# Computing the low halves of the second MLP's weights on VectorE in place of GpSimd

## The chip, the cores and the metric

The kernel runs on one core of one Trainium2 chip. The metric is the device time of one execution in microseconds (us), less is better; a kernel's number is the median of several runs.

## The reference

Three layers follow each other. The first is banded attention, with a window of 32 keys in half of the heads and a dilated window in the others. The second is a maxout MLP, the third an MLP with a rational activation. All is in float32.

```python
attn = softmax(where(mask, q @ k.T / 8, -1e9)) @ v      # 4 x 8 heads, 576 x 64 each
x = attn as (2304, 512)
h = maximum(maximum(x @ w1, x @ w2), x @ w3)            # 512 -> 768
x2 = h @ w_out                                          # 768 -> 512
h = x2 @ w_in                                           # 512 -> 2048
g = (a0 + a1*h + a2*h**2 + a3*h**3) / (1 + |b0|*|h| + |b1|*h**2 + 1e-6)
out = g @ w_out2                                        # 2048 -> 512
```

## The kernel before

To keep the precision, every matrix of the two MLPs is split into a high half, rounded to a format that TensorE takes at full rate, and a low half, the rest. A product is three matmuls: high by high, high by low, low by high. `mm3` (L497 to L499) issues such triples.

The tokens of the attention and the first MLP go in six units of 384 tokens (`TU`). While TensorE does the first MLP of unit u (`moe1`, L502), the pieces of the attention of unit u+1 are put between its groups. A group is 12 matmuls into one of three PSUM banks; ScalarE copies the first of three groups out (L514), VectorE takes the maximum with the second and third (L516), and then ScalarE writes the high half hh (L520) and VectorE the low half hl (L521). The result goes through xs (L530) to the DRAM tile x2d (the transfer of L531 is issued by GpSimd).

During those units the weights of the second MLP are converted from the input's 64-bit words to float32 and put into the DRAM tiles w2d. In the last unit they come back and are split. That is `load_w2` (L537): a transfer on SP's queue into one of five slots w2r (L542), a copy on ScalarE that makes the high half of the weight tile w2s (L544), and a subtraction that makes the low half (L545). It is called 32 times: five times at the start of the last unit, three times after each of the six f groups of the first MLP (into memory that the weights of that group leave free), and nine times at the end (into memory that the rest of the first MLP leaves free). `load_x2` (L550) brings one of the six blocks of 384 tokens of x2 from x2d into x2r (L552, on SP's queue), and `split_x2` (L556) splits it on ScalarE (L558) and VectorE (L559).

The second MLP goes in 96 slices: six blocks of tokens by sixteen slices of 128 of the 2048 columns. For each slice, `stage_h` makes h in one of five PSUM tiles (12 matmuls, L497 to L499 again, with w2s and x2h, x2l). `act_a` (L718 to L720, ScalarE) and `dve_a` (L725, L727, L728, VectorE) read it; L728 is the last reader of the PSUM tile. `act_b` (L734, L735) and `dve_b` (L740, L742, L744) finish the rational function, `act_c` (L750) and `dve_c` (L755) split it into gh and gl, and `stage_o` (L767 to L769) adds nine matmuls to the output.

The order on each engine is set by a scheduler that works through priorities: the program's order, apart from stretches that are marked as later ones (`load_w2` in the last unit by 300 places, `load_x2` and `split_x2` by 200). Each engine then takes its instructions strictly in that order, and each of them waits for what it needs.

Of the kernel before, what the change touches and what calls it, by code (L numbers as in the profile page):

```python
# [7 lines left out]
F32 = mybir.dt.float32  # L8
# [84 lines left out]
def kernel(  # L93
# [17 lines left out]
    nc = tc.nc  # L111
# [425 lines left out]
    def load_w2(pool):  # L537
        i = n2[0]
        n2[0] += 1
        _, side, c = order2[i]  # L540
        r = w2r_p.tile([128, 512], F32, tag="w2r", bufs=W2R, name="w2r")
        nc.sync.dma_start(out=r, in_=w2d[i])  # L542
        t = pool.tile([128, 1024], F32R, tag=f"w2_{i}", name=f"w2s{i}")
        nc.scalar.activation(out=t[:, 0:512], in_=r, func=AF.Copy)  # L544
        nc.gpsimd.tensor_sub(t[:, 512:1024], r, t[:, 0:512].bitcast(F32))  # L545
        w2s[side, c] = t

    x2 = {}
# [12 lines left out]
    with ExitStack():  # L561
# [69 lines left out]
        for u in range(NU):  # L631
            last = u == NU - 1
            pieces = attn(u + 1) if not last else iter(())
            if last:
                while cv:
                    cv_tick(len(conv_seq))
                cv_es[0].close()
                at_es.close()
                x2_p = ctx.enter_context(
                    tc.tile_pool(name="x2", bufs=1, side="right", reuse_waits="tile"))  # L640
                w2r_p = ctx.enter_context(
                    tc.tile_pool(name="w2r", bufs=1, side="right", reuse_waits="tile"))
                w2a = ctx.enter_context(
                    tc.tile_pool(name="w2a", bufs=1, side="right", reuse_waits="tile"))
                with tc.high_priority(offset=-LATE_X2):
                    load_x2(0)
                with tc.high_priority(offset=-LATE_W2):
                    for _ in range(W2A):
                        load_w2(w2a)
            slot = 0  # L650
            groups = moe1(u)
            while True:
                if u == 0:
                    cv_tick(n_w1)
                    while cv_at["lo"] < (n_w1 if slot >= 3 * F1 else slot + AHEAD):
                        cv_tick(n_w1)
                group = next(groups, None)
                if group is None:
                    break
                kind, f, j = group  # L660
                slot += 1
                if u == 0:
                    pass
                elif not last:
                    tick += 1
                    if tick * TICK // 88 > (tick - 1) * TICK // 88:
                        with tc.high_priority(offset=-LATE_CV):
                            cv_tick(len(conv_seq))
                next(pieces, None)
                if last:  # L670
                    if slot in (8, 10, 12, 14):
                        with tc.high_priority(offset=-LATE_X2):
                            split_x2(0, (slot - 8) // 2)
                    if kind == "h" and j == 2:
                        w1_es[f].close()
                        w2b = ctx.enter_context(
                            tc.tile_pool(name=f"w2b{f}", bufs=1, side="right",
                                         reuse_waits="tile"))
                        with tc.high_priority(offset=-LATE_W2):
                            for _ in range(3):  # L680
                                load_w2(w2b)
# [14 lines left out]
        while n2[0] < len(order2):  # L696
            load_w2(w2c)
# [83 lines left out]
        for g in range(NSL + 3):  # L781
            t, c = divmod(g, F2)
# [122 lines left out]
```

## Time and profile before

| what | value |
|---|---|
| median of three runs | 824.51 us (822.74 to 827.67) |
| the profiled execution's own time | 822.7 us |
| its span, first to last instruction | 820.9 us |
| mean granted TensorE clock | 0.987 of full speed |
| TensorE busy | 801.5 us |
| VectorE busy | 612.2 us |
| ScalarE busy | 486.6 us |
| GpSimd busy | 81.7 us |

In the rows below PE is TensorE's matmuls, PEld its weight loads, DVE is VectorE, ACT ScalarE, POOL GpSimd, SP the engine that issues most transfers; a q behind a name is the engine's sequencer. L545 is line 545 of the kernel. Times are in us from the start of the span unless a column says ns. An arrow in brackets names what ended the idle time ahead of an instruction.

### The profile page before, as it was taken

The numbers are of one execution on the slowest core, as the hardware profiler recorded it, in microseconds if no ns is written. First come the engines' busy times: TensorE is split into PE (matmuls) and PEld (weight loads), VectorE is DVE, ScalarE is ACT, GpSimd is POOL, SyncE is SP. The second block draws the span as 40 slices with busy tenths as digits, with TensorE's granted clock in tenths as the row PEclk, the third lists the DMA queues.
The fourth block names the chain that finished last, engine by engine and source line by source line (L and its number), as shares of the span: only waits on it lengthen the run. The fifth ranks groups of instructions, "written<-read, shape, count | busy, mean of one in ns | idle before, by whom it ended". The sixth has DMA issues, their size and how long they took to land.

```text
span 820.9 us, 13079 instructions
## 1 busy us (share of the span) xinstructions
PE 801.5 (98%) x4965; PEld 745.0 (91%) x4965; DVE 612.2 (75%) x1152; ACT 486.6 (59%) x1023; POOL 81.7 (10%) x109
## 2 busy tenths in 40 slices
PE   7899999999999999999989999999999999999998
PEld 5699999999999999998978899999999999999996
DVE  3589666565566566544199899999999999998996
ACT  3677533333333333255378787787788778777775
POOL 0000000100110110048440000000000000000000
PEclk9699999999999999999989999999999999999999
DMA  8787336565465544426410011011002001000001
GB/s 264 243 315 254 121 122 194 183 197 167 154 191 164 162 153 142 153 68 210 153 52 1 0 40 39 1 40 39 1 1 78 1 0 39 1 2 28 11 1 39
DMA packets 29439, 82.54 MB, mean 101 GB/s; under 512 B 3904, under 2 KB 7488, under 8 KB 29376
## 3 DMA queue, kind: packets, MB, share of 16 engines
q1 hardware_dynamic: 24080, 64.66, 25.0%
q0 software_dynamic: 5296, 17.04, 5.5%
q8 instruction: 39, 0.64, 0.3%
q14 instruction: 24, 0.20, 0.1%
HBM read 63.87 MB, written 17.83 MB: 100 GB/s over the span
## 4 chain that ended last, share of the span: by engine, by line
PE 90%; DMA 3%; ACT 2%; issue 2%; DVE 1%; POOL 1%; SPq 0%; ACTq 0%; POOLq 0%
PE mm L497 11%; PE mm L498 11%; PE mm L499 11%; PE acc L769 8%; PE acc L767 8%; PE acc L768 8%; PE h L497 8%; PE h L498 8%; PE h L499 8%; PE sc L287 3%; PE tpp L343 2%; PE pv L369 2%; DMA w1r<-in_w_dram 2%; PE pv L363 1%; DMA mk<-in_masks_dram 1%
## 5 line engine op out<-in xcount | busy, mean ns | idle before, releaser
L497 PE MATMUL mm<-x1h,w1s 128*128 128x384 f32 x432 | 147.9, 344 | 1.8 <-ACT m L514 0.9
L498 PE MATMUL mm<-x1l,w1s 128*128 128x384 f32 x432 | 145.9, 338 | 1.0 <-DVE x1l L385 1.0
L499 PE MATMUL mm<-x1h,w1s 128*128 128x384 f32 x432 | 145.3, 336 | 0.0
L497 PE MATMUL h<-x2h,w2s 128*128 128x384 f32 x384 | 130.3, 339 | 3.8 <-DVE p L728 3.8
L498 PE MATMUL h<-x2l,w2s 128*128 128x384 f32 x384 | 130.4, 340 | 0.0
L499 PE MATMUL h<-x2h,w2s 128*128 128x384 f32 x384 | 130.3, 339 | 0.0
L767 PE MATMUL acc<-w2s,gh 128*128 128x512 f32 x288 | 113.7, 395 | 0.0
L768 PE MATMUL acc<-w2s,gh 128*128 128x512 f32 x288 | 113.4, 394 | 0.0
L769 PE MATMUL acc<-w2s,gl 128*128 128x512 f32 x288 | 110.3, 396 | 0.0
L718 ACT ACTIVATE q<-h 128x384 f32<-128x384 f32 x96 | 47.2, 492 | 79.2 <-PE h L499 76.9
L725 DVE SCALAR_TENSOR_TENSOR q<-q,cs,ab 128x384 f32<-128x384 f32 x96 | 67.8, 706 | 29.4 <-ACT ab L719 29.3
L497 PEld LDWEIGHTS mm<-x1h,w1s 128*128 128x128 f32 x432 | 81.3, 189 | 3.0 <-ACT m L514 1.3
L498 PEld LDWEIGHTS mm<-x1l,w1s 128*128 128x128 f32 x432 | 81.6, 189 | 2.3 <-DVE x1l L385 2.3
L499 PEld LDWEIGHTS mm<-x1h,w1s 128*128 128x128 f32 x432 | 81.4, 188 | 0.0
L497 PEld LDWEIGHTS h<-x2h,w2s 128*128 128x128 f32 x384 | 73.1, 190 | 8.0 <-DVE p L728 4.1
L498 PEld LDWEIGHTS h<-x2l,w2s 128*128 128x128 f32 x384 | 72.9, 190 | 3.8
L499 PEld LDWEIGHTS h<-x2h,w2s 128*128 128x128 f32 x384 | 73.0, 190 | 0.3
L516 DVE TENSOR_TENSOR m<-mm,m 128x384 f32<-128x384 f32 x72 | 39.9, 555 | 41.1 <-PE mm L499 34.7
L769 PEld LDWEIGHTS acc<-w2s,gl 128*128 128x128 f32 x288 | 54.2, 188 | 11.9
L720 ACT ACTIVATE p<-h,cs 128x384 f32<-128x384 f32 x96 | 65.0, 677 | 0.0
L734 ACT ACTIVATE r<-q,cs 128x384 f32<-128x384 f32 x96 | 59.6, 620 | 5.2 <-DVE q L725 4.7
L768 PEld LDWEIGHTS acc<-w2s,gh 128*128 128x128 f32 x288 | 54.2, 188 | 9.3
(86 smaller groups left out, 1492.7 us busy)
## 6 DMA issues: line engine op xcount, KB each, us to landing
w1r<-in_w_dram SPq DMA_DIRECT2D x18, 512.0 KB, 7.7
raw<-in_w_in_dram SPq DMA_DIRECT2D x16, 512.0 KB, 3.7
w2d<-cvt POOLq DMA_DIRECT2D x32, 256.0 KB, 3.0
raw<-in_w_out_dram SPq DMA_DIRECT2D x16, 512.0 KB, 3.7
w2r<-w2d SPq DMA_DIRECT2D x32, 256.0 KB, 3.1
qTp<-in_qp_dram SPq DMA_DIRECT2D x12, 384.0 KB, 4.1
qTd<-in_qd_dram SPq DMA_DIRECT2D x12, 384.0 KB, 4.6
x2d<-xs POOLq DMA_DIRECT2D x24, 192.0 KB, 2.6
```

The costliest lines, as they stand in the source:

```text
L287: nc.tensor.matmul(scs[n // G][:, n % G, :], lhsT=lq, rhs=rk, start=not pem, stop=not pem or n % G == G - 1)
L497: nc.tensor.matmul(o, lhsT=lh, rhs=rh, start=(i == 0), stop=False)
L498: nc.tensor.matmul(o, lhsT=lh, rhs=rl, start=False, stop=False)
L499: pe_at[0] = nc.tensor.matmul(o, lhsT=ll, rhs=rh, start=False, stop=(i == n - 1))
L516: nc.vector.tensor_tensor(out=t, in0=o, in1=t, op=ALU.max)
L718: nc.scalar.activation(out=s["q"], in_=s["h"], func=AF.Square)
L720: nc.scalar.activation(out=s["p"], in_=s["h"], func=AF.Identity, scale=cs[:, 3:4], bias=cs[:, 2:3])
L725: nc.vector.scalar_tensor_tensor(out=s["q"], in0=s["q"], scalar=cs[:, 5:6], in1=s["ab"], op0=ALU.mult, op1=ALU.add)
L734: nc.scalar.activation(out=s["r"], in_=s["q"], func=AF.Ln, scale=LS, bias=cs[:, 6:7])
L767: nc.tensor.matmul(o, lhsT=gh, rhs=w[:, 0:512], start=(c == 0), stop=False)
L768: nc.tensor.matmul(o, lhsT=gh, rhs=w[:, 512:1024], start=False, stop=False)
L769: nc.tensor.matmul(o, lhsT=gl, rhs=w[:, 0:512], start=False, stop=(c == F2 - 1))
```

## The change

The subtraction that makes the low half of a weight tile of the second MLP is issued on VectorE instead of on GpSimd. Nothing else is edited; the scheduler orders the instructions anew.

```diff
@@ -542,7 +542,7 @@
         nc.sync.dma_start(out=r, in_=w2d[i])
         t = pool.tile([128, 1024], F32R, tag=f"w2_{i}", name=f"w2s{i}")
         nc.scalar.activation(out=t[:, 0:512], in_=r, func=AF.Copy)
-        nc.gpsimd.tensor_sub(t[:, 512:1024], r, t[:, 0:512].bitcast(F32))
+        nc.vector.tensor_sub(t[:, 512:1024], r, t[:, 0:512].bitcast(F32))
         w2s[side, c] = t
```

## Rows read from the trace of the kernel before

**Rows 1.** The page's busy times (busy us, share, instructions) and its chain.
```profile
PE 801.5 (98%) x4965; PEld 745.0 (91%) x4965; DVE 612.2 (75%) x1152; ACT 486.6 (59%) x1023; POOL 81.7 (10%) x109
...
PE 90%; DMA 3%; ACT 2%; issue 2%; DVE 1%; POOL 1%; SPq 0%; ACTq 0%; POOLq 0%
```

**Rows 2.** Windows: length, busy us of PE, PEld, DVE, ACT, POOL, clock, DMA.
```profile
355.00:408.00 53.00, 50.97 (x290) 49.97 (x291) 22.24 (x28) 23.78 (x48) 32.77 (x26) 1.00 0.51 157
...
420.00:422.00 2.00, 0.00 (x0) 0.00 (x0) 1.97 (x4) 1.01 (x3) 0.54 (x1) 0.81 0.00 0
422.00:424.00 2.00, 1.87 (x6) 1.87 (x7) 1.96 (x5) 2.00 (x4) 0.00 (x0) 0.50 0.04 8
```

**Rows 3.** Timeline of TensorE (start, duration, what), 407 to 431.
```profile
407.76 0.34 PE L497 MATMUL h<-x2h,w2s 128*128 128x384 f32 x1
...
417.99 0.34 PE L499 MATMUL h<-x2h,w2s 128*128 128x384 f32 x1
422.13 0.69 PE L497 MATMUL h<-x2h,w2s 128*128 128x384 f32 x1 [3.80 <-DVE p L728]
...
428.06 0.35 PE L497 MATMUL h<-x2h,w2s 128*128 128x384 f32 x1
...
429.46 0.39 PE L767 MATMUL acc<-w2s,gh 128*128 128x512 f32 x1
...
430.16 0.40 PE L769 MATMUL acc<-w2s,gl 128*128 128x512 f32 x1
```

**Rows 4.** VectorE: timeline 411 to 428, and L725's group over the span.
```profile
411.94 9.02 DVE L725 SCALAR_TENSOR_TENSOR q<-q,cs,ab 128x384 f32<-128x384 f32 x1 [14.05 <-ACT ab L719]
420.88 0.55 DVE L727 TENSOR_TENSOR p<-h,p 128x384 f32<-128x384 f32 x1
...
427.09 0.55 DVE L755 TENSOR_TENSOR gl<-p,gh 128x384 fp32r<-128x384 f32 x1
...
L725 DVE SCALAR_TENSOR_TENSOR q<-q,cs,ab 128x384 f32<-128x384 f32 x96 | 67.8, 706 | 29.4 <-ACT ab L719 29.3
```

**Rows 5.** Timeline of GpSimd, 380 to 421.
```profile
380.39 10.98 POOL L545 TENSOR_TENSOR w2s<-w2r,w2s 128x512 fp32r<-128x512 f32 x8 [3.56 <-ACT w2s L544]
...
409.30 11.24 POOL L545 TENSOR_TENSOR w2s<-w2r,w2s 128x512 fp32r<-128x512 f32 x9
```

**Rows 6.** L521 and L516, 355 to 410 (ns: minimum/median/maximum; first, last start).
```profile
L521 DVE TENSOR_TENSOR hl<-m,hh x6: 558/1292/1641, 365.8 to 396.6; 128x384 fp32r<-128x384 f32 x6
...
L516 DVE TENSOR_TENSOR m<-mm,m x12: 545/557/558, 359.9 to 395.5; 128x384 f32<-128x384 f32 x12
```

**Rows 7.** Lines L545 and L480 over the span, the same columns.
```profile
L545 POOL TENSOR_TENSOR w2s<-w2r,w2s x32: 1250/1290/1611, 359.9 to 419.3; 128x512 fp32r<-128x512 f32 x32
...
L480 DVE TENSOR_TENSOR w1s<-cvt,w1s x18: 647/686/694, 27.7 to 81.7; 128x512 fp32r<-128x512 f32 x18
```

**Rows 8.** Timelines of SP, TensorE and ScalarE, 373 to 381.
```profile
373.07 0.52 SPq L552 DMA_DIRECT2D x2r<-x2d  x1
...
375.28 0.45 PE L497 MATMUL mm<-x1h,w1s 128*128 128x384 f32 x1 [0.93 <-ACT m L514]
...
378.02 1.77 ACT L558 ACTIVATE x2h<-x2r 128x384 fp32r<-128x384 f32 x4 [2.80 <-DMA x2r<-x2d]
...
380.60 0.45 PE L497 MATMUL mm<-x1h,w1s 128*128 128x384 f32 x1 [0.86 <-DVE m L516]
```

**Rows 9.** Waits (total us, times, longest us) from 335, and w2r's landing times.
```profile
ACT w2s L544 <- DMA w2r<-w2d: 7.8, 5, 2.3
...
SPq L542 <- POOL w2s L545: 56.1, 26, 16.3
...
DMA to landing us min/median/max: 2.6/3.1/6.4
```

**Rows 10.** Timeline of ScalarE, the last of 32 high halves.
```profile
417.12 0.63 ACT L544 ACTIVATE w2s<-w2r 128x512 fp32r<-128x512 f32 x1
```

## The prediction

> **What bounds the kernel now.** First the page's busy shares and chain [rows 1]: TensorE is busy for 801.5 of 820.9 us and owns 90% of the chain that ended last. So a change on VectorE or GpSimd moves the time only where TensorE stands still or runs slowly. The next view is the windows around the hand-over between the two MLPs [rows 2]. From 355 to 408 TensorE is busy for 50.97 of 53 us; in 420 to 422 it does nothing, and then its clock is granted at 0.50, the 1.2 GHz level of the two (1.2 and 2.4).
>
> The timeline of TensorE shows the hole [rows 3]. The second MLP's first matmul starts at 407.76, the sixtieth (five slices of 12) at 417.99, so full-speed spacing is 10.23 / 59 = 0.173 us. The next starts at 422.13, released by VectorE's L728, the last reader of slice 0's PSUM tile (there are five such tiles). From there 18 matmuls take until 428.06, 0.329 us each. After that the spacing is the full-speed one again.
>
> Why was L728 late? On VectorE, L725 of slice 0 starts at 411.94 and lasts 9.02 us, where the other 95 average (67.8 - 9.02) / 95 = 0.62 [rows 4]. On GpSimd, nine subtractions run without a break from 409.30 to 420.54 [rows 5], and L725 ends 0.42 us after them. Other VectorE instructions with two SBUF inputs suffer too: L521 in this stretch has a median of 1.29 us and a maximum of 1.64 against a minimum of 0.56, while L516, one of whose inputs is in PSUM, keeps 0.55 to 0.56 [rows 6]. GpSimd's eight in a row from 380.39 took 10.98 / 8 = 1.37 each, the nine only 11.24 / 9 = 1.25 [rows 5]: there VectorE got turns in between, here none. I read this as the two engines excluding each other while both read SBUF.
>
> The Trainium skill's "SBUF — State Buffer", section "Who interferes with whom", says that a VectorE instruction with two SBUF inputs contends with a GpSimd one that reads SBUF, and that the one issued first keeps the shared ports for its whole instruction while the second blocks. By that rule L725 should have waited for one subtraction, not for seven; the sum by it is that of the second rival below. The trace agrees for L521 and not for L725.
>
> **Step 1, the hole at 418.** Without GpSimd's subtractions L725 takes 0.62 and slice 0's tile is free by about 414, before TensorE asks for it at 418.2. Removed: 422.13 - 417.99 - 0.17 = 3.97 us of standstill, and 5.93 - 18 x 0.173 = 2.81 us of half clock [rows 3]; together 6.8.
>
> **Step 2, what VectorE takes over.** It gets 32 subtractions of 128x512. L480 does the same on the same shape and types in 0.686 us at the median, against 1.29 on GpSimd [rows 7]; 32 x 0.686 = 22 us. All but the nine above, 23, fall into 355 to 408: 15.8 us on top of 22.2 busy (which the exclusion inflates), 38 of 53 [rows 2]. The cover is TensorE's 51 us of matmuls there; if it went, all 15.8 would count. The other nine, 6.2 us, come after 409.3, because their tiles lie in memory that the first MLP frees last. By the first low half of the output, VectorE must also do 14 instructions, from L725 to L755 of slice 0; 12 of these steps took from 420.88 to 427.09, 0.52 us each [rows 4], so 7.3 us. 409.3 + 6.2 + 7.3 = 422.8. Three stage-a groups wait for ScalarE; apart from the long wait of 14.05 these waits sum to 29.3 - 14.05 over 95, 0.16 us each [rows 4], 0.5 for three: 423.3. TensorE reaches the output matmuls after 84 at 407.76 + 84 x 0.173 = 422.3 and wants the low half with the fourth of them, 0.7 us later as from 429.46 to 430.16 [rows 3], so at 423.0. Given back: 0.3 us, between 0 (VectorE hides all) and 6.0 (the first rival). I take 0.3, as each of its terms is a row of just these instructions.
>
> **Step 3, two smaller holes.** TensorE stood 0.93 us at 375.28, behind ScalarE's L514, and 0.86 at 380.60, behind VectorE's L516 [rows 8]. ScalarE's copies of the high halves wait for w2r transfers, 7.8 us in five waits; SP issues those only when a subtraction frees one of five slots, and waits 56.1 us for GpSimd in 26 waits [rows 9]. The second hole hangs on the same slots: SP comes to the x2r load only at 373.07, ScalarE goes on with its data at 378.02, and L516 stands behind that on VectorE [rows 8]. A subtraction on VectorE frees its slot some 0.6 us sooner, eight in a row several us sooner, and SP's queue moves up with them; an issue 1.0 us earlier is enough for the second hole. I take both, 1.8 us; the bounds are 0 and 1.8. Where a slot comes free early, what is late next is the release of the weight tiles by TensorE itself.
>
> **Moved queues.** GpSimd keeps only transfer issues, those of x2d among them, which follow ScalarE's xs and gain nothing. SP's two kinds of load move up. The new wait on VectorE is for ScalarE's L544; behind it stand L516 and stage a, and TensorE waits for both.
>
> **Sum.** The profiled execution took 822.7 (its span is 820.9): 822.7 - 6.8 - 1.8 + 0.3 = 814.4. The median of the three runs, 824.5, is 1.8 above it; for a median I add half of that: **815.3 us**. About 0.5% (4.1 us) is what a measurement of this kernel can tell from no change; the border is 820.4.
>
> **Rivals.**
> *VectorE becomes the late one at the hand-over.* If all nine last subtractions stand before L725 of slice 0 in VectorE's order, it starts after the ninth high half, 417.12 + 0.63 [rows 10], plus 0.69: 418.4. The low half is then ready at 418.4 + 7.3 + 0.5 = 426.2, 3.2 us late, and if the clock falls as it did after 3.97 us of standstill, 2.8 more: 814.4 - 0.3 + 6.0 = 820.1, as a median 821.0. For it: the program asks for these loads ahead of stage a. Against: four of the nine come late, and stage a of slice 0 is ready between them. Chance 0.12.
>
> *L725's wait is not GpSimd's doing beyond one instruction.* Then only 1.25 us of it goes and the rest has a cause that stays: 822.7 - 1.25 - 1.8 = 819.6, as a median 820.5. For it: L521 got through between eight subtractions that ran in a row, in 1.64 at most. Against: L725 ends as GpSimd ends. Chance 0.08.
>
> *Slower: VectorE blocked behind late transfers.* A w2r transfer lands up to 6.4 us after its issue [rows 9], most likely behind an x2r load, whose own data took 4.95 (373.07 to 378.02). Add 0.63 and 0.69, and VectorE is held until 7.7 us after the issue if a subtraction stands ahead of an L516 on its queue. The first MLP has three PSUM banks, so TensorE can run two more groups, 24 x 0.173 = 4.2 us; then it stands 3.5 us and loses 2.8 of clock, 6.3 a time. It decides from the point where a transfer is issued less than 3.5 us before VectorE comes to its subtraction. Twice makes 814.4 + 12.6 = 827.0, as a median 827.9. For it: the hole of 0.86 us is this pattern in small, behind x2r [rows 8]. Against: the slots come free sooner. Chance 0.06.
>
> **Numbers.** Forecast 0.74. Faster by over 0.5%: nearly all of the forecast and half of the second rival, which sits on the border: 0.76. Within 0.5%: the first rival, half of the second and a little of the forecast: 0.18. Slower: 0.06. Range 813 to 822: below, both savings with nothing given back and no offset (814.1), less 1 us for the scatter of the runs; above, the first two rivals with 1 us for the same. The third is left out.
>
> **What would show it.** Right: no L725 above 1 us, L521 near 0.56 throughout, no TensorE gap and no clock of 0.50 between 418 and 428, 32 subtractions of 0.69 us on VectorE, x2r issued before 372. Wrong: a TensorE gap of over 2 us at the first output matmuls, released by L755 (first rival); an L725 that still lasts several us (second); L516 waiting for L544 with TensorE idle behind it (third). What would make the forecast fail as a whole is an order of instructions on VectorE that the trace of before can't show.

## The result, and the profile after

The changed kernel takes **814.33 us** (median of four runs, 814.25 to 815.14) against 824.17 for the kernel before beside it (822.74 to 827.67). The ratio is 0.9877, with a 95% interval from 0.9857 to 0.9897: 9.8 us, 1.2%, faster. The forecast was 815.3, in a range of 813 to 822. The profiled execution is the one of 815.14 us; its span is 813.4, its mean granted clock 0.991.

First the page's busy times and its chain, to be set beside [rows 1].

```profile
PE 800.1 (98%) x4965; PEld 745.1 (92%) x4965; DVE 614.1 (76%) x1184; ACT 487.9 (60%) x1023; POOL 39.2 (5%) x77
...
PE 96%; ACT 1%; DVE 1%; DMA 1%; issue 0%; SPq 0%; POOL 0%; ACTq 0%
```

VectorE has 32 instructions more and GpSimd 32 fewer, yet VectorE is busy for only 1.9 us more (614.1 for 612.2): its subtractions cover 21.0 us, and what it no longer spends is for the most part time in which its instructions had stood kept waiting, counted as busy: 8.7 us at L725 (67.8 to 59.1, as its group below shows), 4.0 at L521 and 3.9 at L559. TensorE's share of the chain went from 90% to 96%.

The windows of [rows 2], on the kernel after:

```profile
355.00:408.00 53.00, 52.76 (x345) 52.39 (x341) 28.47 (x51) 25.95 (x51) 2.18 (x5) 1.00 0.48 159
420.00:422.00 2.00, 2.00 (x12) 1.94 (x12) 2.00 (x5) 1.97 (x5) 0.00 (x0) 1.00 0.01 4
422.00:424.00 2.00, 2.00 (x10) 1.66 (x9) 2.00 (x5) 2.00 (x6) 0.00 (x0) 1.00 0.00 0
```

TensorE is busy throughout at the hand-over, and the granted clock stays at 1.00, the 2.4 GHz level, where it had been 0.50. Next VectorE's timeline at the hand-over, which answers to [rows 4], with the first low half of the output, L755:

```profile
408.24 3.10 DVE L545 TENSOR_TENSOR w2s<-w2r,w2s 128x512 fp32r<-128x512 f32 x5 [10.70 <-ACT w2s L544]
411.25 0.61 DVE L725 SCALAR_TENSOR_TENSOR q<-q,cs,ab 128x384 f32<-128x384 f32 x1
411.78 0.55 DVE L727 TENSOR_TENSOR p<-h,p 128x384 f32<-128x384 f32 x1
412.41 0.69 DVE L545 TENSOR_TENSOR w2s<-w2r,w2s 128x512 fp32r<-128x512 f32 x1
413.02 0.61 DVE L728 SCALAR_TENSOR_TENSOR p<-p,co,h 128x384 f32<-128x384 f32 x1
...
421.18 0.55 DVE L755 TENSOR_TENSOR gl<-p,gh 128x384 fp32r<-128x384 f32 x1
```

L725 of slice 0 takes 0.61 us in place of 9.02. Five of the nine last subtractions stand ahead of it on VectorE, as one block of 3.10 us; the other four come between the steps of stage a. TensorE's timeline at the first output matmuls shows whether that was too much:

```profile
421.38 0.34 PE L499 MATMUL h<-x2h,w2s 128*128 128x384 f32 x1
421.56 0.39 PE L767 MATMUL acc<-w2s,gh 128*128 128x512 f32 x1
...
422.73 0.63 PE L769 MATMUL acc<-w2s,gl 128*128 128x512 f32 x2
```

L755 ends at 421.18 + 0.55 = 421.73, and TensorE comes to the first matmul that reads gl at 422.73: 1.0 us to spare, and no wait. The moved instruction itself, the low halves hl of the first MLP, and L725's group (busy us, mean ns, idle before), to be set beside [rows 6], [rows 7] and [rows 4]:

```profile
L545 DVE TENSOR_TENSOR w2s<-w2r,w2s x32: 679/684/694, 362.9 to 415.9; 128x512 fp32r<-128x512 f32 x32
...
L521 DVE TENSOR_TENSOR hl<-m,hh x6: 547/550/554, 365.6 to 396.4; 128x384 fp32r<-128x384 f32 x6
...
L725 DVE SCALAR_TENSOR_TENSOR q<-q,cs,ab 128x384 f32<-128x384 f32 x96 | 59.1, 615 | 15.5 <-ACT ab L719 15.4
```

L521 is back at 0.55 in all six cases. SP's queue, to be set beside [rows 8], and ScalarE's wait of [rows 9]:

```profile
369.73 0.53 SPq L552 DMA_DIRECT2D x2r<-x2d  x1
...
ACT w2s L544 <- DMA w2r<-w2d: 2.9, 3, 1.2
```

The x2r load is issued at 369.73, 3.3 us sooner, and the waits for w2r fell from 7.8 to 2.9 us.

**Where the 9.8 us went.** To see it by stage, cut the span at three places: the first L498 of the last unit (TensorE waits there for VectorE's L385), the first matmul of the second MLP, and the issue of the first output transfer (L779). The lengths in us, each from one profiled execution; those of the experiments belong to the sections below:

| kernel | first MLP, last unit | hand-over and first block | rest |
|---|---|---|---|
| before | 51.02 | 80.55 | 332.6 |
| after | 48.66 | 73.75 | 332.6 |
| last nine on VectorE | 51.50 | 73.75 | 333.0 |
| first 23 on VectorE | 48.64 | 79.27 | 332.6 |
| every subtraction twice | 48.65 | 80.12 | 332.6 |
| L725 reads PSUM | 52.12 | 75.59 | 332.4 |
| memset behind each subtraction | 48.68 | 76.30 | 333.1 |

The change took 6.80 us out of the hand-over and 2.36 out of the last unit, 9.16 together. The two profiled executions differ by less, 822.7 - 815.1 = 7.6, since the last unit began 1.6 us later in the one of after (358.33 for 356.74), ahead of the first subtraction. That is scatter and not the change: in the seven executions of the table it began anywhere from 356.66 to 358.33, and at 356.66 in the kernel that has every subtraction on VectorE twice. The medians differ by 9.84.

The last unit's windows, from its first matmul that waits to the second MLP's first, of the kernel before:

```profile
356.74:407.76 51.02, 49.23 (x280) 48.54 (x281) 21.32 (x26) 22.95 (x46) 32.77 (x26) 1.00 0.52 161
```

and of the kernel after:

```profile
358.33:406.99 48.66, 48.66 (x280) 48.66 (x281) 27.05 (x49) 23.49 (x46) 1.62 (x3) 1.00 0.51 169
```

The same 280 matmuls now run without a gap; VectorE does its 23 further subtractions, 15.8 us, in 5.73 us more of busy time, and none of it is seen by TensorE.

### The profile page after: what moved, and what is told of

The parts are those of the page before. It is cut to its first block, busy times and chain, and to the rows that moved or that the text cites. A ratio compares the mean times of both kernels' runs of the same rounds, so it can differ in the third digit from the quotient of the medians.

```text
span 813.4 us, 13081 instructions
## 1 busy us (share of the span) xinstructions
PE 800.1 (98%) x4965; PEld 745.1 (92%) x4965; DVE 614.1 (76%) x1184; ACT 487.9 (60%) x1023; POOL 39.2 (5%) x77
## 4 chain that ended last, share of the span: by engine, by line
PE 96%; ACT 1%; DVE 1%; DMA 1%; issue 0%; SPq 0%; POOL 0%; ACTq 0%
PE mm L498 12%; PE mm L497 12%; PE mm L499 12%; PE h L498 8%; PE acc L769 8%; PE h L499 8%; PE h L497 8%; PE acc L767 8%; PE acc L768 8%; PE sc L287 4%; PE tpp L343 2%; PE pv L369 2%; PE pv L363 1%; DMA mk<-in_masks_dram 1%; ACT x1h L384 1%; PE warmth L604 0%
## 5 line engine op out<-in xcount | busy, mean ns | idle before, releaser
L498 PE MATMUL mm<-x1l,w1s 128*128 128x384 f32 x432 | 146.0, 338 | 1.0 <-DVE x1l L385 1.0
L498 PE MATMUL h<-x2l,w2s 128*128 128x384 f32 x384 | 129.2, 337 | 0.0
L499 PE MATMUL h<-x2h,w2s 128*128 128x384 f32 x384 | 129.0, 336 | 0.0
L497 PE MATMUL h<-x2h,w2s 128*128 128x384 f32 x384 | 128.9, 336 | 0.0
L498 PEld LDWEIGHTS mm<-x1l,w1s 128*128 128x128 f32 x432 | 81.6, 189 | 2.2 <-DVE x1l L385 2.2
L497 PEld LDWEIGHTS h<-x2h,w2s 128*128 128x128 f32 x384 | 72.1, 188 | 3.9
L498 PEld LDWEIGHTS h<-x2l,w2s 128*128 128x128 f32 x384 | 72.0, 188 | 3.8
L499 PEld LDWEIGHTS h<-x2h,w2s 128*128 128x128 f32 x384 | 72.1, 188 | 0.3
L516 DVE TENSOR_TENSOR m<-mm,m 128x384 f32<-128x384 f32 x72 | 39.9, 554 | 42.2 <-PE mm L499 41.4
L725 DVE SCALAR_TENSOR_TENSOR q<-q,cs,ab 128x384 f32<-128x384 f32 x96 | 59.1, 615 | 15.5 <-ACT ab L719 15.4
L768 PEld LDWEIGHTS acc<-w2s,gh 128*128 128x128 f32 x288 | 54.1, 188 | 9.4
L767 PEld LDWEIGHTS acc<-w2s,gh 128*128 128x128 f32 x288 | 54.0, 188 | 9.0
```

Of the source, the lines that this page charges most:

```text
L497: nc.tensor.matmul(o, lhsT=lh, rhs=rh, start=(i == 0), stop=False)
L498: nc.tensor.matmul(o, lhsT=lh, rhs=rl, start=False, stop=False)
L499: pe_at[0] = nc.tensor.matmul(o, lhsT=ll, rhs=rh, start=False, stop=(i == n - 1))
L516: nc.vector.tensor_tensor(out=t, in0=o, in1=t, op=ALU.max)
L725: nc.vector.scalar_tensor_tensor(out=s["q"], in0=s["q"], scalar=cs[:, 5:6], in1=s["ab"], op0=ALU.mult, op1=ALU.add)
L767: nc.tensor.matmul(o, lhsT=gh, rhs=w[:, 0:512], start=(c == 0), stop=False)
```

## The experiments

Theory: the time lay in two places, GpSimd's last nine subtractions that kept L725 out, and its first 23 that held up the slots of w2r. Rivals: only one instruction's worth of L725's wait was GpSimd's; or it was something of L725 itself. Each kernel below is the kernel before with one edit, unless it says otherwise.

**1. The last nine alone.**

```diff
-        nc.gpsimd.tensor_sub(t[:, 512:1024], r, ...)
+        (nc.vector if i >= 23 else nc.gpsimd).tensor_sub(t[:, 512:1024], r, ...)
```

> Only the last nine low halves move to VectorE; the first 23 stay on GpSimd. Exclusion theory (the hole at 418 is L725 kept out by the nine GpSimd subtractions): the hole and its half clock go, about 7 us faster than before, L725 of slice 0 takes 0.6 us, the two smaller holes at 375 and 380 stay (0.9 us each), 817 us. Rival (the subtractions' speed matters and not which engine excludes which, so that the 23 in the first MLP carry the gain through w2r's slots): at most 2 us faster.

Measured: 818.71 us against 824.11, ratio 0.9942 (0.9920 to 0.9963), 5.4 us. The hand-over is as short as after's, 73.75, and the holes of the last unit stay. TensorE's timeline there:

```profile
376.84 0.44 PE L497 MATMUL mm<-x1h,w1s 128*128 128x384 f32 x1 [1.29 <-ACT m L514]
382.26 0.45 PE L497 MATMUL mm<-x1h,w1s 128*128 128x384 f32 x1 [0.99 <-DVE m L516]
```

These are the two of [rows 8], of 0.93 and 0.86 us. So the whole gain at the hand-over comes from these nine, and none of the gain in the last unit does. The median gained 1.6 us less than the 7 expected; in the profiled execution the last unit and the rest are 0.5 and 0.4 us longer than before, and why was not followed.

**2. The first 23 alone.**

```diff
+        (nc.vector if i < 23 else nc.gpsimd).tensor_sub(t[:, 512:1024], r, ...)
```

> The other part alone: the first 23 low halves on VectorE, the last nine on GpSimd. Exclusion theory: only the two smaller holes go, about 2 us faster than before (822), L725 of slice 0 still lasts 8 to 9 us and TensorE still stands about 4 us and then runs at half clock. Rival (slots carry the gain): 7 us faster.

Measured: 820.23 against 824.11, ratio 0.9951 (0.9934 to 0.9967), 3.9 us. The last unit is as short as after's (48.64). The hand-over was to cost what it did before, and cost 1.3 less: its nine subtractions fell into five and four, because the sixth high half came only at 418.3. GpSimd's timeline:

```profile
408.00 6.28 POOL L545 TENSOR_TENSOR w2s<-w2r,w2s 128x512 fp32r<-128x512 f32 x5
418.38 6.34 POOL L545 TENSOR_TENSOR w2s<-w2r,w2s 128x512 fp32r<-128x512 f32 x4 [4.09 <-ACT w2s L544]
```

and VectorE's:

```profile
410.56 4.16 DVE L725 SCALAR_TENSOR_TENSOR q<-q,cs,ab 128x384 f32<-128x384 f32 x1 [13.63 <-ACT ab L719]
...
419.32 1.19 DVE L744 SCALAR_TENSOR_TENSOR p<-p,co,r 128x384 f32<-128x384 f32 x1
...
420.95 1.10 DVE L740 SCALAR_TENSOR_TENSOR q<-q,r 128x384 f32<-128x384 f32 x1
422.09 1.51 DVE L742 SCALAR_TENSOR_TENSOR r<-q,r 128x384 f32<-128x384 f32 x1
423.52 1.61 DVE L755 TENSOR_TENSOR gl<-p,gh 128x384 fp32r<-128x384 f32 x1
```

and TensorE's waits:

```profile
421.12 0.50 PE L767 MATMUL acc<-w2s,gh 128*128 128x512 f32 x1 [0.53 <-ACT gh L750]
...
425.19 0.73 PE L769 MATMUL acc<-w2s,gl 128*128 128x512 f32 x2 [2.88 <-DVE gl L755]
```

L725 is kept out until the five end (414.28) and ends 0.44 us after them, as it ended 0.42 after the nine. Beside the four, L744 to L755 each get in after one subtraction. Even so those four instructions lost 3.2 us together (5.41 for the 0.55 to 0.61 that each takes alone), gl came late, TensorE stood 2.88 us for it, and its granted clock fell to 0.59 in the 2 us from 426. By the medians the two parts make 5.4 + 3.9 = 9.3 of the 9.8 us. They can't be added more exactly than that: the 1.3 us at the hand-over is counted in both, and their intervals reach from 3.0 to 6.6 and from 2.7 to 5.4 us.

**3. Every subtraction twice, on VectorE.** The kernel after, with L545 issued two times; the second repeats the first.

```diff
         nc.vector.tensor_sub(t[:, 512:1024], r, t[:, 0:512].bitcast(F32))
+        nc.vector.tensor_sub(t[:, 512:1024], r, t[:, 0:512].bitcast(F32))
```

> The changed kernel with each of the 32 subtractions done twice on VectorE (the second writes the same values). This measures the cover of step 2. Theory: 23 extra ones in the first MLP are hidden under TensorE's matmuls (VectorE busy 44 of 53 us); the nine extra ones at the hand-over, 5.5 to 6.2 us, use up the margin of 1.0 us that the first low half has in the changed kernel, so TensorE waits 4.5 to 5 us and, if its clock falls again, some 2.5 more: 4.5 to 8 us slower than the changed kernel, 819 to 822. Rival (VectorE has slack to spare there): within 1 us of the changed kernel.

Measured: 821.02 us, 6.7 above after; its own ratio to before is 0.9957 (0.9942 to 0.9972). In the last unit VectorE was busy for 42.39 of 53 us and the stretch is as long as after's (48.65): 23 further subtractions are hidden there. At the hand-over nothing is. VectorE's timeline:

```profile
411.98 0.61 DVE L725 SCALAR_TENSOR_TENSOR q<-q,cs,ab 128x384 f32<-128x384 f32 x1
412.51 5.50 DVE L545 TENSOR_TENSOR w2s<-w2r,w2s 128x512 fp32r<-128x512 f32 x9
...
418.92 0.60 DVE L728 SCALAR_TENSOR_TENSOR p<-p,co,h 128x384 f32<-128x384 f32 x1
```

and TensorE's wait:

```profile
419.58 0.69 PE L497 MATMUL h<-x2h,w2s 128*128 128x384 f32 x1 [3.70 <-DVE p L728]
```

L728 starts 6.9 us behind L725, in place of 1.8 in the kernel after (411.25 to 413.02), TensorE stands 3.70 us for it, and 80.12 - 73.75 = 6.37 us are lost, nearly what GpSimd's nine had cost. So VectorE becomes the late one at the hand-over, as in the first rival, once it gets nine subtractions more. The wait is another one than the rival and the expectation had, though: TensorE waits for L728 and slice 0's PSUM tile, and the first low half comes in time (L755 ends at 424.91, and the first matmul that reads it starts at 426.10). So this run does not measure the 1.0 us to spare of the kernel after.

**4. L725 with one SBUF input.** L725 takes h from PSUM in place of ab, and a maximum in place of the sum; this leaves the term |b0||h| out of the denominator.

```diff
-                                           in1=s["ab"], op0=ALU.mult, op1=ALU.add)
+                                           in1=s["h"], op0=ALU.mult, op1=ALU.max)
```

> All subtractions stay on GpSimd, but L725 takes h from PSUM as its second input instead of ab from SBUF, and a maximum instead of the sum, so it has one SBUF input only; the term with the absolute value of h is left out of the denominator. Exclusion theory: L725 of slice 0 takes 0.6 us although GpSimd subtracts; the next instruction with two SBUF inputs, L740 of slice 0, is held until GpSimd ends at about 420, so TensorE's standstill before 422 goes or shrinks to under 2 us: 4 to 7 us faster than before. Rival (L725's 9 us have another cause, it being the first of its loop): L725 stays at 9 us and the time at 824.

Measured: 819.14 against 824.11, ratio 0.9936 (0.9909 to 0.9962). GpSimd's timeline, and then VectorE's:

```profile
411.16 11.30 POOL L545 TENSOR_TENSOR w2s<-w2r,w2s 128x512 fp32r<-128x512 f32 x9
```

```profile
414.36 0.61 DVE L725 SCALAR_TENSOR_TENSOR q<-q,cs,h 128x384 f32<-128x384 f32 x1 [14.64 <-ACT p L720]
```

In the middle of the nine L725 now takes 0.61 us, and the hole at 418 is gone, though not one subtraction was moved: 4.96 of the 6.80 us are back (75.59 for 80.55). An L740 that asks at 422.06 still waits for the ninth, and TensorE stands 0.71 us for gh later. So L725 is kept out by its second input from SBUF. That the operation changed with it does not matter: as a plain addition with both inputs in SBUF (experiment 5) it still took 9.02 us. The Trainium skill, "SBUF — State Buffer", section "Who interferes with whom", says that an instruction with at most one SBUF input does not contend with GpSimd, outside the 2-port performance modes: the trace agrees, with 0.61 us in the middle of the row.

**5. Other forms of the same two instructions.** First L725 as a plain addition (the factor |b1| on the square is left out), then L521 as a fused multiply and subtract with the same values.

```diff
-            nc.vector.scalar_tensor_tensor(out=s["q"], in0=s["q"], scalar=cs[:, 5:6],
-                                           in1=s["ab"], op0=ALU.mult, op1=ALU.add)
+            nc.vector.tensor_tensor(out=s["q"], in0=s["q"], in1=s["ab"], op=ALU.add)
...
-                    nc.vector.tensor_sub(hl, t, hh.bitcast(F32))
+                    nc.vector.scalar_tensor_tensor(out=hl, in0=t, scalar=1.0, in1=hh.bitcast(F32),
+                                                   op0=ALU.mult, op1=ALU.subtract)
```

> All subtractions on GpSimd; L725 is a plain tensor_tensor sum of q and ab in place of the scalar_tensor_tensor form (the factor on q is left out, so the denominator is another one). If the form of the instruction is what keeps L725 out through seven subtractions, where L521 (tensor_tensor) got in after one: L725 of slice 0 lasts at most 2 us and 5 to 7 us are gained. If the form plays no part: it lasts 8 to 9.5 us and the time stays within 1 us of before.

> All subtractions on GpSimd; L521, the low half of the first MLP's h, is written as a scalar_tensor_tensor (times 1.0, minus hh) in place of tensor_tensor; values are the same. If the form is what keeps an instruction out: L521 lasts 5 to 10 us at 382 and 367, L516 behind it is late and TensorE stands several us more, time above 828. If the form plays no part: L521 stays at 1.0 to 1.7 us next to GpSimd and the time within 1 us of before.

Measured: 823.16 against 823.90, ratio 0.9997 (0.9971 to 1.0024), and 823.84, ratio 0.9996 (0.9973 to 1.0018). L725 still takes 9.02 us as an addition; L521 has 558/1277/1630 ns for the 558/1292/1641 of [rows 6]. The form plays no part.

**6. L725 issued behind L727 and L728 in the program.**

```diff
-            nc.vector.scalar_tensor_tensor(out=s["q"], ...)
             nc.vector.tensor_mul(s["p"], s["h"], s["p"])
             nc.vector.scalar_tensor_tensor(out=s["p"], ...)
+            nc.vector.scalar_tensor_tensor(out=s["q"], ...)
```

> All subtractions on GpSimd; stage a on VectorE is turned round, L727 and L728 (one SBUF input, h from PSUM) first and L725 (two SBUF inputs) last, so that slice 0's PSUM tile does not hang on L725, and L725 does not come after 14 us of idling. If any instruction with two SBUF inputs is kept out as long as GpSimd's subtractions follow each other without a break: L725 of slice 0 lasts 7 to 9 us again, TensorE stands about 2 us at 420 in place of 4 at 418 and waits again for the first low half; 1 to 4 us faster than before. If only an instruction that comes after VectorE has been idle is kept out so long: L725 lasts at most 2 us, and 5 to 7 us are gained.

Measured: 823.65 against 823.90, ratio 0.9982 (0.9961 to 1.0003). The scheduler put slice 0's L725 first all the same, and it took 9.02 us again. The edit did not do what it was meant to do, so it says nothing.

**7. A pause behind each subtraction.** GpSimd writes one column of the used w2r tile after each.

```diff
+        nc.gpsimd.memset(r[:, 0:1], 0.0)
```

> All subtractions stay on GpSimd, but a GpSimd memset of one column (about 0.1 us) stands after nearly each of them, so that the nine at the hand-over no longer run back to back. If VectorE gets its turn in a gap between two GpSimd instructions that read SBUF: L725 of slice 0 lasts at most 2 us (one or two subtractions), and about 5 to 7 us are gained. If an instruction of L725's form gets no turn until GpSimd has no subtraction left: L725 stays at 8 to 10 us and the time at 824 or a little above.

Measured: 817.84 against 824.11, ratio 0.9924 (0.9892 to 0.9956). GpSimd's timeline:

```profile
412.07 1.28 POOL L545 TENSOR_TENSOR w2s<-w2r,w2s 128x512 fp32r<-128x512 f32 x1
413.30 0.09 POOL L545 MEMSET w2r<- 128x1 f32 x1
413.36 1.28 POOL L545 TENSOR_TENSOR w2s<-w2r,w2s 128x512 fp32r<-128x512 f32 x1
414.58 0.21 POOL L545 MEMSET w2r<- 128x1 f32 x2
```

L725 asked at 410.87 and ended at 415.07, 4.20 us, which neither side of the expectation had (at most 2, or 8 to 10): memsets of 0.1 us did not let it in, and it came in at the first place where GpSimd spent 0.21 us on them. Whether it was the longer pause is not shown, for at that place the next high half also came late: ScalarE finished the sixth at 414.15, while the fifth subtraction ran (from 413.36), and in the kernel before at 413.97, ahead of the fifth (at about 414.3, going by nine in 11.24 us from 409.30). The edit also moved SP's queue (x2r was issued at 366.73, and the last unit's holes are gone with it), so the time is not the pause's alone.

**8. What lets VectorE in?** L725 is kept out through seven subtractions, yet L521 and others get in after one. The next two kernels ask whether it was VectorE's idling ahead of it (14.05 us in [rows 4]). VectorE copies slice 0's h four times into a spare tile first; in the second, L725 takes its factor from that tile.

```diff
+            ... [nc.vector.tensor_copy(dm, s["h"]) for _ in range(4)] ...
```

> GpSimd's subtractions as before. Ahead of the L725 of slice 0 VectorE copies that slice's PSUM tile four times into a spare tile (one PSUM input, 0.5 to 0.6 us each), and the scheduler puts L727 ahead of L725 as well, so that VectorE has not stood idle when L725 comes to its turn, at about 413, in the middle of GpSimd's nine subtractions. Theory A: what let L725 wait through seven subtractions is that VectorE had stood idle for 14 us before it; then L725 lasts at most 1.7 us here like the other instructions that got in, the hole at 418 is gone, and the time is 5 to 7 us below before. Theory B: subtractions whose inputs are ready before the one ahead of them ends keep the other engine out, whatever that engine did before; then L725 still lasts about 7 to 8 us and ends 0.4 us after the ninth subtraction, and the time is within 1 us of before.

> The run before missed its end: the scheduler put the four copies behind the first L725. Now slice 0's L725 takes its factor from the spare tile that the copies write (the last of them puts the same factor there), so the copies come first on VectorE, then L727, then two L725 one after the other, the first of them at about 413 to 414 with at most 1 us of idle time ahead of it, in the middle of GpSimd's nine subtractions, which stay as they were. Theory A: what let L725 wait through seven subtractions is that VectorE had stood idle for 14 us before it; then the first L725 lasts at most 1.7 us here, slice 0's PSUM tile is free by about 417, the hole at 418 is gone, and the time is 4 to 7 us below before. Theory B: subtractions whose inputs are all ready keep the other engine out, whatever that did before; then the first L725 lasts 6 to 8 us, ends 0.4 us after the ninth subtraction, and the time is within 1 us of before.

Measured: 826.44 against 824.49, ratio 1.0017 (0.9993 to 1.0040); the copies came behind L725, which took 9.02 again: a miss. Then 823.82 against 824.27, ratio 1.0005 (0.9980 to 1.0031), with this on VectorE:

```profile
412.67 2.33 DVE L725 COPY dm<-h 128x384 f32<-128x384 f32 x4 [14.61 <-ACT p L720]
414.93 0.55 DVE L727 TENSOR_TENSOR p<-h,p 128x384 f32<-128x384 f32 x1
415.39 0.14 DVE L725 COPY dm<-cs 128x1 f32<-128x1 f32 x1
417.59 3.54 DVE L725 SCALAR_TENSOR_TENSOR q<-q,cs,ab 128x384 f32<-128x384 f32 x1 [2.06 <-ACT ab L719]
```

The first L725 came later than meant, with 2.06 us of idle time ahead of it, and was still kept out, through the two subtractions that were left, until 0.42 us after the ninth (420.71). In the kernel before, an L521 with 5.67 us of idle time ahead of it got in after one subtraction (1.32 us, at 374.37). So how long VectorE had merely stood idle does not decide it.

**9. Instructions of another kind ahead of L725, and a single one.** First 24 subtractions of x2h from x2r into the spare tile, 128x384 like L521, given to VectorE ahead of stage a (slice 0's L725 takes its factor from the tile again); then, in another kernel, a single one, which reads the second high half of the last nine.

```diff
+            ... [nc.vector.tensor_sub(dm, x2[0][0][:, 0, :], x2[0][1][:, 0, :].bitcast(F32)) for _ in range(24)] ...
...
+            load_w2(w2c); nc.vector.tensor_sub(wk.tile(...), w2s[order2[22][1:]]..., w2s[order2[n2[0] - 1][1:]]...) if n2[0] == 25 else None
```

> GpSimd's subtractions as before. Ahead of slice 0's L725 VectorE is given 24 subtractions of x2h from x2r into a spare tile (128x384, two SBUF inputs: the kind of L521 and of L559, both of which got in between GpSimd's subtractions after one). The scheduler puts eight of them behind the last L521, with nothing of GpSimd's beside them, then L727 of slice 0, then one, L728, one, then an L725, and so on, so that the first of them behind L727 (at about 413) and the one behind L728 meet GpSimd's nine subtractions ahead of any L725. Theory L: it is something of L725 itself (its tiles, or their having just been written by ScalarE) that keeps it out; then the two last at most 1.7 us each, L728 comes before 417, and the L725 behind them lasts until 0.4 us after the ninth subtraction. Theory H: the nine at the hand-over keep any VectorE instruction with two SBUF inputs out; then the first of the two lasts about 7 to 8 us and ends 0.4 us after the ninth. The time is over before's by 1 to 6 us in either case, for the added work.

> All subtractions stay on GpSimd, and every queue keeps its order; VectorE gets one extra instruction (128x384, two SBUF inputs, into a spare tile) that waits for the second high half of the last nine, and so comes to its turn while the first of GpSimd's nine subtractions runs, some 2.3 us ahead of slice 0's L725. Theory T: in the traces so far VectorE was kept out only where GpSimd had done two or more subtractions in a row, without a pause and without a turn of VectorE's, before VectorE asked; so the extra instruction gets in after the first subtraction (at most 1.7 us), the second is held for it, L725 asks with none or one done since and lasts at most 1.7 us in place of 9.02, and the hole of 3.97 us at 418 is gone; the time is 3 to 7 us below before, with less than the whole if a later instruction that asks after two more subtractions is kept out in its turn. Theory N: a single turn changes nothing, since it was VectorE's steady asking from before the nine that kept its place in the last run; then the extra instruction or L725 still lasts until 0.4 us after the ninth subtraction, 8 us or more, and the time is within 1 us of before.

Measured, the first: 831.51 us in one run against 824.45 (the added reads also hold x2r longer, which put later x2r loads back on SP's queue). Memory for the spare tile came free only at 405.96, so eight of the added instructions ran from there into GpSimd's first two subtractions. Neither theory holds: everything got in. GpSimd's timeline, then VectorE's:

```profile
409.90 13.21 POOL L545 TENSOR_TENSOR w2s<-w2r,w2s 128x512 fp32r<-128x512 f32 x9
```

```profile
413.57 0.90 DVE L725 TENSOR_TENSOR dm<-x2r,x2h 128x384 f32<-128x384 f32 x1
414.39 0.60 DVE L728 SCALAR_TENSOR_TENSOR p<-p,co,h 128x384 f32<-128x384 f32 x1
414.92 1.12 DVE L725 TENSOR_TENSOR dm<-x2r,x2h 128x384 f32<-128x384 f32 x1
417.97 0.89 DVE L725 SCALAR_TENSOR_TENSOR q<-q,cs,ab 128x384 f32<-128x384 f32 x1 [1.93 <-ACT ab L719]
418.79 1.64 DVE L725 TENSOR_TENSOR dm<-x2r,x2h 128x384 f32<-128x384 f32 x1
```

Here GpSimd's nine were held instead (13.21 us for 11.24), and an L725 got in within 0.89. The second: 824.08 against 824.18, ratio 1.0005 (0.9983 to 1.0026). VectorE's timeline:

```profile
410.51 11.42 DVE L697 TENSOR_TENSOR dm<-w2s,w2s 128x384 f32<-128x384 f32 x1 [11.66 <-ACT w2s L544]
421.85 0.60 DVE L725 SCALAR_TENSOR_TENSOR q<-q,cs,ab 128x384 f32<-128x384 f32 x1
```

The single instruction asked during the first of the nine (they ran from 410.29 to 421.51) and was itself kept out through all of them. Theory T falls: it did not matter that GpSimd had finished none of its row. Being kept out is nothing of L725's own either, since an instruction of another kind suffered it and an L725 escaped.

**What stays open.** With every run in hand I set side by side each VectorE instruction with two SBUF inputs that ran past the end of at least one of GpSimd's subtractions, 123 in the kernel before and the eleven others that leave subtractions on GpSimd. Nine of them were kept out beyond one subtraction. In all nine, the high half for GpSimd's next subtraction was already there when VectorE asked, and VectorE had had no such instruction in the 11 us before. Where VectorE got in after one and another followed, either that high half came only after it had asked, or VectorE had had such an instruction under 2 us before; two L521 fit neither (at 374.59 in the first kernel of experiment 8, and at 370.56 in experiment 7, with a memset behind the subtraction). It is a pattern found afterwards, and no run was made to test it. What decides who comes next is not settled.

## Why the prediction was right

**The bound** was read rightly: TensorE, slowed only at the hand-over and in two small holes. Both parts of the gain are where the prediction put them, and experiments 1 and 2 show them apart.

**Step 1, the hole at 418.** Predicted 6.8 us, 3.97 of standstill and 2.81 of half clock. The stretch of the hand-over became 80.55 - 73.75 = 6.80 shorter, with nothing given back. The reading that L725 waits for GpSimd is shown by experiment 4, which cures it without moving a subtraction, and the second rival (one instruction's worth) falls with it and with experiment 1. Why it waits for the whole row and not for one subtraction, the prediction took from the row as it stood, and the runs leave it open.

**Step 2, what VectorE takes over.** The price was right, 0.684 us for each in place of 0.686. So was the cover of the 23 (experiment 3 puts twice as many under it). Of the give-back of 0.3 us, nothing came. The low half was forecast 423.3 - 407.76 = 15.5 us after the second MLP's first matmul, and was there after 421.73 - 406.99 = 14.7: the very 9 + 14 instructions were done, and they took 13.5 us from 408.24, waits included, for the 14.0 of the sum, from a start 0.3 us sooner. TensorE wanted it later, 422.73 - 406.99 = 15.7 us after for the 15.2 of the forecast, since the first matmul that reads it was the sixth of the output and not the fourth. So 0.3 us too late became 1.0 us in time. The first rival, nine ahead of L725, did not come about: five were ahead and four between. With nine more, VectorE does become the late one (experiment 3), though TensorE then waits for L728 and not for the low half.

**Step 3, the small holes.** Both went, and x2r was issued 3.3 us sooner, where 1.0 was wanted; counted from the start of the last unit it was issued after 11.4 us in place of 16.3. The other kernels speak for SP's queue as the way: in the eight that issue x2r 16.3 to 16.4 us after that start, all with these subtractions on GpSimd, both holes stand, and they are gone where it is issued after 11.3 (experiment 2) and after 8.7 (experiment 7, with every subtraction on GpSimd). An early issue is not the only way, though: in experiment 3 x2r is issued only after 22.0 us, ScalarE comes to its data later as well (at 383.93), and there is no hole. The worth of the holes was mis-sized. The idle column, 0.93 + 0.86 = 1.79, is not what a hole costs; the stretch became 2.36 us shorter. For the same 280 matmuls TensorE's busy time fell by 0.57 (49.23 to 48.66): ahead of a hole the last matmul is drawn with its whole 0.33 us, and after it the first with 0.44, while a new one starts every 0.173 us in a full stream. Step 1 had counted from start to start, and had no such error.

**Sum.** With 2.36 for 1.8 and 0 for 0.3, and the rest kept: 822.7 - 6.8 - 2.36 + 0.9 = 814.4, against 814.33 measured. The 0.9, half of the median's distance from the profiled execution, was an allowance, and what lies behind that distance was not followed. So close a sum is in part luck: the profiled execution that the forecast starts from was the fastest of the four of before, and the one of after was the slowest of its four.

**The slower rival**, VectorE blocked behind a late transfer, did not come about in the four runs. Its mechanism exists: in the profiled execution of the kernel with L521 in another form (829.64 us, GpSimd still subtracting) the x2r load was issued at 375.78 and ScalarE had its data at 383.33, 7.55 us later in place of 4.95 [rows 8], and TensorE's timeline has this.

```profile
385.90 0.44 PE L497 MATMUL mm<-x1h,w1s 128*128 128x384 f32 x1 [3.48 <-DVE m L516]
```

It is the second hole of [rows 8], four times as long. In the kernel after, with x2r issued 3.3 us sooner, no such hole is in the profiled execution; that it can no longer come was not shown.

## What to carry to other kernels

Moving work from GpSimd to a busier VectorE can free both, where GpSimd's instructions and VectorE's have two inputs in SBUF: look for VectorE instructions whose maximum stands far above their minimum, and see whether they end just after a row of GpSimd's. Price such a move by stage: under TensorE's stream the 23 subtractions cost nothing here, even at twice the amount; between the last transfers and the first output matmuls nine were hidden, and nine more cost 6.4 us. Count a hole from start to start of the matmuls around it, and add the time that TensorE then spends at the lower granted clock.

## What the runs showed of the hardware

A row of nine GpSimd subtractions kept one VectorE instruction out for 9.02 us in five kernels, and for 11.42 in a sixth, where one subtraction lasts 1.25. The wait spanned two to eight further subtractions, while in other places the two engines took turns. The prediction set the rule of the Trainium skill, "SBUF — State Buffer", section "Who interferes with whom" (the one that comes second waits for the other's whole instruction), against the first such row, and the runs bear out the row: the waits went through up to nine instructions and not one. Short work between, 0.1 us on GpSimd, did not end it; it ended once where that work took 0.21 us, and where the next high half came late too. Whether a VectorE instruction that asks steadily keeps its turn, as in the run with 24, is what a further test should ask.
